# Attention transposes in pairs of 64-row halves, into pairs of PSUM banks, and table clears three stages later

## The chip, the cores and the metric

One core of a Trainium2 chip runs one launch. The metric is device microseconds of that launch; a time is the median of several runs of the same program. The engines are TensorE (PE in the profile; its weight loads are listed apart as PEld), VectorE (DVE), ScalarE (ACT), GpSimd (POOL) and SyncE (SP), which only issues DMAs here.

## The reference

Three layers follow each other. Attention has 2 batches, 8 heads, 576 positions and head size 64, with a relative bias made by a small network; then a mixture of 8 experts of which each token takes one, with a capacity of 288; then a feed-forward layer with a leaky gate.

```python
scores = scale * np.matmul(q, k.transpose(0, 1, 3, 2)) + bias.transpose(2, 0, 1)[None]
attn = np.exp(scores - np.max(scores, axis=-1, keepdims=True))
attn = attn / (np.sum(attn, axis=-1, keepdims=True) + 1e-09)
x = np.matmul(attn, v)                       # -> (1152, 512), all heads side by side
logits = x @ w_gate; expert_idx = np.argmax(logits, axis=1)
h = np.maximum(np.einsum('ecd,edf->ecf', disp, w1), 0.0)
y = np.einsum('ecf,efd->ecd', h, w2)         # rows go back to their tokens, times a gate
h = x @ w_in
out = (np.maximum(h, 0.0) + alpha * np.minimum(h, 0.0)) @ w_out
```

## The kernel before

Everything is float32. Attention is cut into units: a batch, a pair of heads `hp`, and one or two blocks of 128 query rows (`uls`); the last 64 rows of both heads of a pair make a small unit. `SL` lists 24 stages of units: stages 0 to 3 are small units, 4 to 11 single units (one block), 12 to 23 double units (two blocks a and b; at stages 12, 13, 18 and 20 a small unit stands ahead in the list). In the double stages no bias work is left; the single and small ones carry two blocks of it each (`bias_mm`, `bias_out`).

`course` (L886) writes out the order of TensorE, ScalarE and VectorE by hand (`manual_schedule`). In stage s it runs the scores of unit u of this stage and the transposes and values of unit w of the stage before:

- `scores` (L227): matmuls of 64 rows each, the two heads in the two 64-row halves of the array, 288 columns each, into two PSUM tiles of the pool `pq` (two buffers of two banks). A float32 matmul shows as two weight loads and two matmuls.
- `low` (L250, VectorE): adds the bias, writes the exponent's argument to SBUF and its row minimum; it releases the PSUM tile.
- `expo` (L258, ScalarE): the exponential, with the row sum.
- `turn` (L272): TensorE transposes blocks of 128 x 128 (9 blocks of keys for each block of rows: 4 of head 0, one in the middle that holds the end of both heads, 4 of head 1) into a one-bank tile of the pool `pt`, and returns the copy of it to `PT` in SBUF by ScalarE ('A') or VectorE ('D').
- `values` (L292): probabilities times values, 64-column tiles, into the pool `pa`, and VectorE's copy to `xT`.

In a double stage the order is: scores of a, their two `low`; the transposes of w (18 blocks in five tiles, three copied by ScalarE, two by VectorE) and those of a waiting small unit (5 blocks in two tiles); a step of `late`; `expo` of a, scores of b, and their `low`; values; `expo` of b; a step; the scores, `low` and `expo` of a small unit of this stage; a step. `late` is a list of the work that follows attention, by steps: from stage 18 on the first batch's routing (`logits` to `gates`), `row` (L450: four transposes give 128 tokens' rows of x, VectorE scales them), `scatter`, `second` (gathers the first expert's rows and loads its weights), `first_halves` and `rows_in` (L878: transposes the gathered rows).

PSUM has eight banks: `pq` four, `pt` three tiles of one bank, `pa` one. `pt` also takes the tiles of routing and rows. `LD` lists what SP loads at which stage: bias tables, keys/queries/values (`load`, four buffers), and `clear` (L117), which stores zeros to the table of scattered rows (four stores) and to the output (three), one at each of stages 14 to 20. The scatter waits for the first four. SP's, POOL's and the later engines' order outside `course` is made by a scheduler.

Of the kernel before, what the change touches and what calls it, by code (L numbers as in the profile page):

```python
# [10 lines left out]
F32 = mybir.dt.float32  # L11
# [4 lines left out]
ALU = mybir.AluOpType  # L16
AX = mybir.AxisListType
ET = mybir.EngineType
PSUM = bass.MemoryType.PSUM
# [20 lines left out]
def build(tc, nc, a):  # L40
    V, A, G, T, SY = nc.vector, nc.scalar, nc.gpsimd, nc.tensor, nc.sync
    with contextlib.ExitStack() as ctx:
        left, right = contextlib.ExitStack(), contextlib.ExitStack()

        def pool(stack, name, bufs=1, **k):
            return stack.enter_context(tc.tile_pool(name=name, bufs=bufs, **k))
# [9 lines left out]
        pt = pool(banks, "pt", 3, space=PSUM)  # L56
        pa = pool(banks, "pa", 1, space=PSUM)
        ps1 = lambda p, name, *s: p.tile([128, *(s or (512,))], F32, tag="pt" if p is pt else "pa", name=name)
# [151 lines left out]
        def unit(b, hp, *uls):  # L210

            u = Unit()
            u.b, u.hp, u.small, u.uls = b, hp, not uls, uls
            return u
# [51 lines left out]
        def copy(e, o, i):  # L266
            if e == 'A':
                A.copy(o, i)  # L268
            else:
                V.tensor_copy(o, i)  # L270

        def turn(u, *js):  # L272

            if u.small:
                t = ps1(pt, "t1", 4, 128)
                if js[0] == 0:
                    u.PT = ap.tile([128, 5, 128], F32, tag="pt4", name="pt4", bufs=2)
                    for j in range(4):
                        T.transpose(t[:, j], u.P[:, 128 * j:128 * j + 128], ident)
                    return lambda: copy('A', u.PT[:, 0:4], t)  # L280
                T.transpose(t[:, 0], u.dup.rearrange("p a b -> p (a b)"), ident)
                return lambda: [copy('D', u.PT[p, 4, 0:64], t[p, 0, p]) for p in halfs]
            n = 128 * len(u.uls)
            if js[0] == 0:
                u.PT = ap.tile([128, 9, 256], F32, tag="PT", name="PT")
            t = ps1(pt, "t1", 512 // n, n)
            for jl, j in enumerate(js):
                for i, ul in enumerate(u.uls):
                    T.transpose(t[:, jl, 128 * i:128 * i + 128], u.P[ul][:, 128 * j:128 * j + 128], ident)  # L289
            return lambda e: copy(e, u.PT[:, js[0]:js[-1] + 1, :n], t[:, 0:len(js)])  # L290
# [57 lines left out]
        def routing(b):  # L348
# [101 lines left out]
            def row(u):  # L450
                t = ps1(pt, "xp")
                for hp in range(4):
                    T.transpose(t[:, 128 * hp:128 * hp + 128], xT[b][:, hp, 128 * u:128 * u + 128], ident)
                x = r.x[u] = raw.tile([128, RW], F32, tag="xr", name="xr", bufs=5)
                V.tensor_tensor(x[:, 0:DM].rearrange("p (h d) -> p h d", h=8), t.rearrange("p (h d) -> p h d", h=8),
                                r.rinv[:, u].unsqueeze(2).to_broadcast([128, 8, 64]), ALU.mult)
                V.tensor_copy(x[:, DM:RW], r.gt[:, u])

            def scatter():
                for u in range(5):  # L460
# [7 lines left out]
                    + tuple(lambda u=u: row(u) for u in range(5)) + (scatter,))]  # L468
# [417 lines left out]
        def course():  # L886
# [31 lines left out]
            for s in range(14, 21):  # L918
                LD[s].append((clear, 3 * s - 42))
# [18 lines left out]
            for s in range(NU + 1):  # L938
# [11 lines left out]
                if u is None or len(u.uls) == 2:  # L950
# [31 lines left out]
                else:  # L982
# [4 lines left out]
                    if w and w.small:  # L987
                        turn(w, 0)()
                        turn(w, 4)()
# [29 lines left out]
        banks.close()  # L1019
        pt = pool(ctx, "pt", 2, space=PSUM)  # L1020
# [194 lines left out]
```

## Time and profile before

| | us |
|---|---|
| median of 3 runs | 391.95 (390.59 to 392.08) |
| profiled execution | 392.17 |
| its span, first to last instruction | 390.1 |
| TensorE matmul busy | 364.9 |
| VectorE busy | 280.2 |
| ScalarE busy | 233.3 |

The span is what the trace covers; the execution's own time lies a little above it. Busy matmul time counts a matmul from its start to its modelled end, and matmuls overlap, so the pace of a group is read from the distance of starts and not from the length of one.

### The profile page before, as it was taken

The page shows a single profiled execution, that of the slowest core. Times are in us where ns is not written, and L with a number is a line of the kernel's source. Part 1 is how long each engine was busy: PE and PEld are TensorE (multiplying, and loading weights), DVE is VectorE, ACT ScalarE, POOL GpSimd, SP SyncE. Part 2 cuts the span into 40 slices and gives each one's busy share as a digit, 9 for nine tenths or more (in the row PEclk, how much of TensorE's full clock was granted, in tenths as well). Part 3 has the DMA queues.
Part 4 walks back from the last instruction along what each step waited for, and adds up shares of the span by engine and source line. Part 5 has one row for each costly group of instructions (what it writes and reads, how often), then busy time and mean ns, then how long its engine had stood idle before and what let it go on. Part 6 is the DMA issues. An engine that isn't in the chain of part 4 may idle for free. (4 is left out here: it accounts for less than half of the span.)

```text
span 390.1 us, 7650 instructions
## 1 busy us (share of the span) xinstructions
PE 364.9 (94%) x2784; PEld 272.4 (70%) x2785; DVE 280.2 (72%) x680; ACT 233.3 (60%) x525; POOL 29.8 (8%) x48
## 2 busy tenths in 40 slices
PE   4989999999999999899999988999999999999993
PEld 2424566666666657577669877778889898988982
DVE  5988868746566656867759898216999999879430
ACT  4877798886566644555754326334866765755531
POOL 1000000000000000023022340002000000000004
PEclk9999999999999999999999999999999999999997
DMA  7898996789999960520765199483454755550003
GB/s 311 228 282 295 363 294 202 256 274 360 313 357 361 402 228 0 186 102 9 229 170 181 52 279 347 133 276 103 159 172 152 215 163 163 163 164 1 0 2 134
DMA packets 44011, 78.79 MB, mean 202 GB/s; under 512 B 7127, under 2 KB 21591, under 8 KB 43964
## 3 DMA queue, kind: packets, MB, share of 16 engines
q1 hardware_dynamic: 42780, 75.73, 60.3%
q0 software_dynamic: 1184, 2.48, 1.7%
q8 instruction: 24, 0.39, 0.4%
q14 instruction: 23, 0.19, 0.2%
HBM read 59.50 MB, written 20.09 MB: 204 GB/s over the span
## 5 line engine op out<-in xcount | busy, mean ns | idle before, releaser
L254 DVE CUSTOM_DVE_ANT_0 p<-sps,bias 128x576 f32<-128x576 f32 x72 | 52.0, 755 | 26.5 <-PE sps L247 12.7
L261 ACT ACTIVATE p<-p,mn 128x576 f32<-128x576 f32 x72 | 56.0, 781 | 23.3 <-DVE mn L254 23.3
L247 PE MATMUL sps<-kqv 64*128 64x288 f32 x256 | 47.9, 432 | 2.5 <-DVE mn L254 1.9
L171 DVE TENSOR_SCALAR h<-c 128x528 f32<-128x528 f32 (+17 forms) x126 | 46.4, 443 | 0.2
L179 PE MATMUL bps<-h,c 128*32 128x512 f32 (+17 forms) x352 | 36.1, 498 | 7.7 <-DVE h L171 5.5
L289 PE MATMUL t<-ident,p 128*128 128x128 f32 x288 | 39.1, 281 | 1.2 <-ACT PT L268 0.9
L289 PEld LDWEIGHTS t<-ident,p 128*128 128x128 f32 x288 | 30.7, 141 | 12.5 <-issue 5.8
L268 ACT COPY PT<-t 128x512 f32<-128x512 f32 (+2 forms) x59 | 25.6, 506 | 21.1 <-PE t L289 21.1
L247 PEld LDWEIGHTS sps<-kqv 64*128 64x128 f32 x256 | 26.0, 185 | 16.2 <-issue 4.2
L819 PE MATMUL fg<-yh,w1l 128*128 128x304 f32 x120 | 36.3, 302 | 0.0
L819 PE MATMUL fg<-yh,w1h 128*128 128x304 f32 x120 | 36.3, 302 | 0.0
L819 PE MATMUL fg<-yl,w1h 128*128 128x304 f32 x120 | 36.2, 302 | 0.0
L187 ACT ACTIVATE st<-bps,c 128x527 f32<-128x527 f32 (+35 forms) x72 | 31.2, 515 | 4.4 <-PE bps L179 4.4
L310 PE MATMUL av<-PT,kqv 128*64 128x256 f32 (+1 forms) x320 | 32.8, 343 | 0.0
L744 ACT ACTIVATE cv<-d 128x512 f32<-128x512 f32 x32 | 21.6, 674 | 16.0 <-DMA d<-in_wout 5.4
L310 PEld LDWEIGHTS av<-PT,kqv 128*64 128x64 f32 x320 | 19.7, 136 | 14.9 <-issue 5.2
L831 PE MATMUL facc<-w2h,hl 128*128 128x512 f32 (+1 forms) x75 | 29.7, 396 | 0.0
L831 PE MATMUL facc<-w2l,hh 128*128 128x512 f32 (+1 forms) x75 | 29.6, 394 | 0.0
L831 PE MATMUL facc<-w2h,hh 128*128 128x512 f32 (+1 forms) x75 | 29.5, 394 | 0.0
L179 PEld LDWEIGHTS bps<-h,c 128*32 128x32 f32 x352 | 12.6, 114 | 23.8 <-DVE h L171 7.8
L514 ACT CAST hh<-g 128x304 fp32r<-128x304 f32 x32 | 14.3, 446 | 15.8 <-DVE g L823 15.8
L819 PEld LDWEIGHTS fg<-yh,w1h 128*128 128x128 f32 x120 | 22.6, 188 | 1.0
(200 smaller groups left out, 743.4 us busy)
## 6 DMA issues: line engine op xcount, KB each, us to landing
bias<-bd SPq DMA_DIRECT2D x24, 576.0 KB, 6.3
kqv<-in_kqv SPq DMA_DIRECT2D x14, 864.0 KB, 7.0
bd<-st SPq DMA_DIRECT2D x36, 295.5 KB, 5.7
raw<-in_ew SPq DMA_DIRECT2D x16, 512.0 KB, 6.9
d<-in_win SPq DMA_DIRECT2D x16, 512.0 KB, 3.8
d<-in_wout SPq DMA_DIRECT2D x16, 512.0 KB, 3.4
w<-in_ew SPq DMA_DIRECT2D x6, 512.0 KB, 8.8
xd<-zr SPq DMA_DIRECT2D x4, 722.8 KB, 10.2
```

What stands on the lines that cost most here:

```text
L171: V.tensor_scalar(h, tab[:, :n], psi[:, i:i + 1], 0.0, ALU.add, ALU.max)
L179: T.matmul(ps[32 * c:32 * c + 32, n0:n1], w2n, hs[c][:, n0:n1], start=True, stop=True)
L187: A.activation(st[:, o:o + src.shape[1]], src, AF.Copy, scale=rr[:, t:t + 1])
L247: T.matmul(u.sc[ul, h][0][:, nh, :288], q[p, 128 * ul:128 * ul + 128], k[p, 288 * nh:288 * nh + 288], start=True, stop=True)
L254: V.tensor_tensor_reduce(out.rearrange("p (a b) -> p a b", a=2), ps[:, :, :288], bias.rearrange("p (a b) -> p a b", a=2), -0.125, 3.0e38, ...
L261: A.activation(out, out, AF.Exp, bias=mn, scale=-1.0, accum_out=acc)
L268: A.copy(o, i)
L289: T.transpose(t[:, jl, 128 * i:128 * i + 128], u.P[ul][:, 128 * j:128 * j + 128], ident)
L310: T.matmul(o[p, c], v[:, j, p], rhs(h, j), start=j == 0, stop=False, skip_group_check=True)
L744: A.mul(v, r[:, :, 1].bitcast(F32), 2.0 ** -112)
L819: T.matmul(ps, w[:, 128 * k:128 * k + 128], x[:, k, s], start=k + i == 0, stop=k + i == 5)
L831: T.matmul(acc[i][:m], h[:, r:r + m], w, start=f == 0 and j == 0, stop=f == NF - 1 and j == 2)
```

## The change

`turn` transposes each 128 x 128 block as two halves of 64 rows, with a 64 x 64 identity; half h goes to bank h of a tile of two banks. So the array is tiled as for the scores. The tiles are one pool now, `pt` and `pa` being the same ring of two buffers of two banks. In a double stage the middle keys come first (ScalarE copies them), then keys 0 to 3 and keys 5 to 8, of which ScalarE copies half 0 and VectorE half 1. ScalarE's first exponential of a stands between these copies. The small unit's transposes, in one tile of five blocks, and the first step of `late` come after the scores of b. `row` of the first batch uses the same halves, rows 0 and 1 and rows 3 and 4 in one tile each, and moves by a step or two in `late`. The seven clears go to stages 17 to 23.

```diff
-        pt = pool(banks, "pt", 3, space=PSUM)
-        pa = pool(banks, "pa", 1, space=PSUM)
+        pt = pa = pool(banks, "pt", 2, space=PSUM)
+        packed = True
+        ps2 = lambda name: pt.tile([128, 2, 512], F32, tag="pt", name=name)
+
+        def ps1(p, name):
+            if packed:
+                return ps2(name)[:, 0]
+            return p.tile([128, 512], F32, tag="pt" if p is pt else "pa", name=name)
...
+            t = ps2("t1")
...
+                rows = [u.P[ul][:, 128 * j:128 * j + 128] for j in js for ul in u.uls]
+            for i, x in enumerate(rows):
+                for h, p in enumerate(halfs):
+                    T.transpose(t[:, h, 64 * i:64 * i + 64], x[p], ident[p, p])
+            src = t[:, :, 0:64 * len(rows)].rearrange("p h (m c) -> p h m c", c=64)
...
+            def out(*es):
+                if len(es) == 1:
+                    copy(es[0], dst, src)
+                else:
+                    for h, e in enumerate(es):
+                        copy(e, dst[:, h], src[:, h])
+            return out
...
-            for s in range(14, 21):
-                LD[s].append((clear, 3 * s - 42))
+            for s in range(17, 24):
+                LD[s].append((clear, 3 * s - 51))
...
                     if len(w.uls) == 2:
-                        for js, e in (((0, 1), 'A'), ((2, 3), 'A'), ((4,), 'A'), ((5, 6), 'D'), ((7, 8), 'D')):
-                            turn(w, *js)(e)
+                        turn(w, 4)('A')
+                        if u:
+                            expo(u, u.uls[0], 0)
+                        turn(w, 0, 1, 2, 3)('A', 'D')
+                        turn(w, 5, 6, 7, 8)('A', 'D')
                     else:
-                        for js, e in (((0, 1, 2, 3), 'A'), ((4,), 'A'), ((5, 6, 7, 8), 'D')):
-                            turn(w, *js)(e)
-                    if wsmall:
-                        turn(wsmall, 0)()
-                        turn(wsmall, 4)()
-                    step()
+                        turn(w, 0, 1, 2, 3, 4)('A')
+                        expo(u, u.uls[0], 0)
+                        turn(w, 5, 6, 7, 8)('A')
                     if u:
-                        expo(u, u.uls[0], 0)
                         scores(u, u.uls[1])
                         expo(u, u.uls[0], 1)
                         low(u, u.uls[1], 0)
                         low(u, u.uls[1], 1)
+                    if wsmall:
+                        turn(wsmall)()
+                    step()
                     c = values(*[z for z in (w, wsmall) if z])
...
-                        turn(w, 0, 1, 2, 3)('A')
-                        turn(w, 4)('A')
+                        turn(w, 0, 1, 2, 3, 4)('A')
                         turn(w, 5, 6, 7, 8)('A')
...
-                    late.extend([[], st[:1], [], st[1:3], st[3:5], [], st[5:7], st[7:8], st[8:9], st[9:11], [], [],
-                                 st[11:13], [], [st[13], st[14], second], [], [first_halves], [], [rows_in]])
+                    late.extend([[], st[:1], [], st[1:3], st[3:5], [], st[5:7], st[7:8], st[8:9], [], st[9:10], [],
+                                 st[10:11], st[11:12], [st[12], second], [], [first_halves], [], [rows_in]])
```

## Rows read from the trace of the kernel before

**Rows 1.** The page: busy us, share of span and instructions of each engine.

```profile
PE 364.9 (94%) x2784; PEld 272.4 (70%) x2785; DVE 280.2 (72%) x680; ACT 233.3 (60%) x525; POOL 29.8 (8%) x48
```

**Rows 2.** Windows: stretch, length, busy PE/PEld/DVE/ACT/POOL (x), clock, DMA share, GB/s.

```profile
79.83:85.51 5.68, 5.68 (x56) 3.48 (x54) 1.74 (x5) 5.06 (x15) 0.00 (x0) 1.00 0.86 260
...
118.83:125.90 7.07, 7.05 (x57) 4.65 (x55) 4.60 (x11) 4.50 (x12) 0.00 (x0) 1.00 1.03 344
...
174.32:182.91 8.59, 8.57 (x70) 5.91 (x66) 6.40 (x17) 4.50 (x11) 1.96 (x2) 1.00 0.08 27
...
199.93:385.50 185.57, 178.10 (x1147) 157.99 (x1144) 140.53 (x290) 99.75 (x211) 17.43 (x18) 1.00 0.50 154
```

**Rows 3.** Single lines' instructions, durations in ns: min/median/max, first to last start.

```profile
L289 PEld LDWEIGHTS t<-ident,p x288: 137/141/146, 48.0 to 192.5; 128*128 128x128 f32 x144
L289 PE MATMUL t<-ident,p x288: 272/273/332, 48.0 to 192.6; 128*128 128x128 f32 x144
...
L247 PE MATMUL sps<-kqv x256: 402/403/507, 41.1 to 187.3; 64*128 64x288 f32 x128
...
L310 PE MATMUL av<-pt,kqv x128: 219/222/270, 32.2 to 174.0; 128*64 128x64 f32 x128
```

**Rows 4.** Timeline, stage 16: start, length, engine, line, tiles, count, [idle before].

```profile
118.83 1.24 PE L247 MATMUL sps<-kqv 64*128 64x288 f32 x8
...
120.00 2.48 PE L289 MATMUL t<-ident,p 128*128 128x128 f32 x18
...
120.20 0.76 DVE L254 CUSTOM_DVE_ANT_0 p<-sps,bias 128x576 f32<-128x576 f32 x1 [0.82 <-PE sps L247]
...
120.88 0.75 DVE L254 CUSTOM_DVE_ANT_0 p<-sps,bias 128x576 f32<-128x576 f32 x1
121.34 0.91 PEld L289 LDWEIGHTS t<-ident,p 128*128 128x128 f32 x8 [0.26 <-ACT PT L268]
...
122.03 1.29 DVE L270 COPY PT<-t 128x512 f32<-128x512 f32 x2 [0.39 <-PE t L289]
...
122.42 1.24 PE L247 MATMUL sps<-kqv 64*128 64x288 f32 x8
...
123.59 1.95 PE L310 MATMUL av<-PT,kqv 128*64 128x256 f32 x16
```

**Rows 5.** Timeline, stage 13 and the start of stage 14.

```profile
92.88 1.24 PE L247 MATMUL sps<-kqv 64*128 64x288 f32 x6 [0.33 <-DVE mn L254]
...
94.47 0.75 DVE L254 CUSTOM_DVE_ANT_0 p<-sps,bias 128x576 f32<-128x576 f32 x1
...
97.19 1.24 PE L247 MATMUL sps<-kqv 64*128 64x288 f32 x8
...
100.57 0.64 PE L310 MATMUL av<-pt,kqv 128*64 128x64 f32 x16
...
101.25 1.19 PE L237 MATMUL sps<-kqv 64*64 64x288 f32 x8
...
103.45 1.23 PE L247 MATMUL sps<-kqv 64*128 64x288 f32 x6 [0.33 <-DVE mn L254]
```

**Rows 6.** Timeline, stage 11, a single stage.

```profile
79.83 1.54 PE L247 MATMUL sps<-kqv 64*128 64x288 f32 x8
...
82.05 1.24 ACT L268 COPY PT<-t 128x512 f32<-128x512 f32 x3 [0.62 <-PE t L289]
```

**Rows 7.** Timeline, stage 24, the end of attention.

```profile
189.98 1.31 PE L289 MATMUL t<-ident,p 128*128 128x128 f32 x10
...
193.20 0.37 PEld L567 LDWEIGHTS xjT<-ident,xj 96*128 96x128 f32 x4 [0.15 <-DVE PT L270]
...
194.28 1.51 PE L310 MATMUL av<-PT,kqv 128*64 128x256 f32 x10
```

**Rows 8.** DMA issues, 111.7 to 126: count, KB each, median us to landing.

```profile
kqv<-in_kqv SPq DMA_DIRECT2D x3, 864.0 KB, 8.7
out<-zr SPq DMA_DIRECT2D x3, 768.0 KB, 10.3
```

More of the change, by code (lines that the diff above doesn't have):

```diff
@@ L55, in build @@
         banks = contextlib.ExitStack()
-        pt = pool(banks, "pt", 3, space=PSUM)
-        pa = pool(banks, "pa", 1, space=PSUM)
-        ps1 = lambda p, name, *s: p.tile([128, *(s or (512,))], F32, tag="pt" if p is pt else "pa", name=name)
+        pt = pa = pool(banks, "pt", 2, space=PSUM)
[5 more added lines that the diff above has]
+            return p.tile([128, 512], F32, tag="pt" if p is pt else "pa", name=name)
         class Table:
@@ L213, in unit @@
             u.b, u.hp, u.small, u.uls = b, hp, not uls, uls
+            u.first = 4 if len(uls) == 2 else 0
             return u
@@ L272, in turn @@
         def turn(u, *js):
+            t = ps2("t1")
             if u.small:
[L275 to L290, printed above, removed]
+                u.PT = ap.tile([128, 5, 128], F32, tag="pt4", name="pt4", bufs=2)
@@ new lines, in turn @@
+                rows = [u.P[:, 128 * j:128 * j + 128] for j in range(4)] + [u.dup.rearrange("p a b -> p (a b)")]
+            else:
+                if js[0] == u.first:
+                    u.PT = ap.tile([128, 9, 256], F32, tag="PT", name="PT")
+                rows = [u.P[ul][:, 128 * j:128 * j + 128] for j in js for ul in u.uls]
+            for i, x in enumerate(rows):
+                for h, p in enumerate(halfs):
+                    T.transpose(t[:, h, 64 * i:64 * i + 64], x[p], ident[p, p])
@@ new lines, in turn, with out @@
+            src = t[:, :, 0:64 * len(rows)].rearrange("p h (m c) -> p h m c", c=64)
+            if u.small:
+                def out():
+                    copy('A', u.PT[:, 0:4].rearrange("p m (h c) -> p h m c", h=2), src[:, :, 0:4])
+                    for h, p in enumerate(halfs):
+                        copy('D', u.PT[p, 4, 0:64], src[p, h, 4])
+                return out
+            dst = u.PT[:, js[0]:js[-1] + 1, :128 * len(u.uls)]
+            if len(u.uls) == 2:
+                dst = dst.rearrange("p j (i h c) -> p h (j i) c", h=2, c=64)
+            else:
+                dst = dst.rearrange("p j (h c) -> p h j c", h=2)
@@ L292, in values @@
+            def out(*es):
+                if len(es) == 1:
+                    copy(es[0], dst, src)
+                else:
+                    for h, e in enumerate(es):
+                        copy(e, dst[:, h], src[:, h])
+            return out
         def values(*us):
@@ L448, in routing, with row @@
             r.x = {}
[L450 to L457, printed above, removed]
+            def row(*us):
+                t = ps2("xp") if packed else ps1(pt, "xp")
+                for i, u in enumerate(us):
+                    x = r.x[u] = raw.tile([128, RW], F32, tag="xr", name="xr", bufs=5)
+                    if packed:
+                        c = 256 * i
+                        for hp in range(4):
+                            for h, p in enumerate(halfs):
+                                T.transpose(t[:, h, c + 64 * hp:c + 64 * hp + 64], xT[b][p, hp, 128 * u:128 * u + 128],
+                                            ident[p, p])
+                        z = x[:, 0:DM].rearrange("p (g h d) -> p h g d", h=2, d=64)
+                        y = t[:, :, c:c + 256].rearrange("p h (g d) -> p h g d", d=64)
+                        w = r.rinv[:, u].rearrange("p (g h) -> p h g", h=2).unsqueeze(3).to_broadcast([128, 2, 4, 64])
+                    else:
+                        for hp in range(4):
+                            T.transpose(t[:, 128 * hp:128 * hp + 128], xT[b][:, hp, 128 * u:128 * u + 128], ident)
+                        z, y = [z.rearrange("p (h d) -> p h d", h=8) for z in (x[:, 0:DM], t)]
+                        w = r.rinv[:, u].unsqueeze(2).to_broadcast([128, 8, 64])
+                    V.tensor_tensor(z, y, w, ALU.mult)
+                    V.tensor_copy(x[:, DM:RW], r.gt[:, u])
             def scatter():
@@ L467, in routing @@
                     (logits, logits_rows, choose, highest, hot, ranks, slots, places, gates)
-                    + tuple(lambda u=u: row(u) for u in range(5)) + (scatter,))]
+                    + tuple(lambda u=u: row(*u) for u in (((0, 1), (2,), (3, 4)) if b == 0 else ((0,), (1,), (2,), (3,), (4,)))) + (scatter,))]
         jl = gp.tile([128, 52], I32, name="jl")
@@ L1019, in build @@
         banks.close()
+        packed = False
         pt = pool(ctx, "pt", 2, space=PSUM)
```

3 lines of the change are left out of this document (1 added, 2 removed).

## The prediction

> **What bounds the kernel now.** I read the page first: TensorE is recorded busy for 94% of the span [rows 1]. Such a number is an average, so next I cut the trace into stages. In the windows view the attention's plain double stage (one unit of two 128-row blocks, no routing) takes 7.07 us with TensorE busy 7.05, VectorE 4.60, ScalarE 4.50, at a granted clock of 1.00 (2.4 GHz) [rows 2]. So these stages are bound by the order of TensorE's own work, and a shorter TensorE step can shorten them until something else is late. The single stages (5.68 us, TensorE 5.68 [rows 2]) look alike, but there the timeline shows ScalarE idle 0.62 us until the transposes arrive [rows 6], and little else of its time free: a loop of ScalarE through TensorE. From 199.93 on, 185.57 us [rows 2] belong to experts and feed-forward, whose code is not touched. I leave them as they are.
>
> Within a double stage the timeline [rows 4] gives, from the scores of block a at 118.83 (call it 0): transposes 1.17 to 3.6, scores of block b from 3.59, values from 4.76, next stage at 7.07.
>
> **What a transpose costs, before and after.** 18 transposes took 2.48 us [rows 4]. The last lasts 0.273, and the first 0.332, some 0.06 over the median, which is its exposed weight load [rows 3]. The reader should separate duration from pace: ten weight loads and eight in two runs, with a wait of 0.2 between them; (0.91 - 0.141)/7 = 0.110 us per transpose [rows 3, 4]. The scores' pairs, already in 64-row halves, stream 288 columns in (1.24 - 0.403 - 0.104)/3 = 0.244 us for two matmuls at once [rows 3, 4]. That is 0.85 ns a column, and 128 columns at 0.85 are 0.109: the transpose is paid by its 128 streamed identity columns, not by its load of about 0.06.
>
> After the change a block is two transposes of 64 rows with 64 streamed columns each. No row shows a transpose in halves. Upper bound: the halves don't overlap and loads aren't hidden, 2 x (0.06 + 0.054) = 0.23 us a block. Middle: they don't overlap but loads hide, 0.11. Lower bound: they overlap as the scores' halves do. The nearest row for that is the small unit's values, pairs of 64-column matmuls with two loads each: 16 in 0.64, so (0.64 - 0.222)/7 = 0.060 a pair [rows 3, 5]. I take 0.060, because the row tiling is that of the scores, whose halves do run together, and because load (0.06) and stream (0.054) both fit.
>
> The tiling stays that of the scores, so the change of tiling disappears on both sides. From the end of the scores' stream (118.83 + 0.104 + 4 x 0.244 = 119.91) to the first transpose's effective start (120.00 + 0.06) there are 0.15 us, and on the other side about 0.2 [rows 4].
>
> **A plain double stage.** TensorE's work alone would shrink by 18 x 0.050 + 0.35 + the 0.2 wait = 1.45 us. It can't all be had. Scores of b need the two PSUM buffers that VectorE's reductions read. Those start at 120.20 and the second ends at 120.88 + 0.75 = 121.63, 2.80 after the stage's start [rows 4]. New sequence: scores of a to 1.08; middle keys (2 blocks) to 1.20; keys 0 to 3 to 1.68; keys 5 to 8 reuse the middle keys' buffer, whose copy ScalarE ends at about 1.9, so they run 1.95 to 2.45 (a new wait of 0.25; behind it on TensorE stand scores of b, which wait longer for VectorE anyway); scores of b not before 2.87 (VectorE); stream end 3.94; values need VectorE's two copies (1.29 together [rows 4]) from 2.81 to 4.10, so they start about 4.16. Before, the values' first effective start was 4.81 (4.76 and a 0.05 load) and the stage ended 2.25 later; 4.16 + 2.25 = 6.41, **0.65 less**. ScalarE's order (middle copy, exponential, two half copies, exponential; a copy of 512 takes it about 0.5, by three in 1.24 [rows 6]) ends its copies at 4.02, just in time. Four such stages (15 to 18): 2.6.
>
> A rule of the Trainium skill, TensorEngine Tiling (Array Packing), PSUM Bottleneck, speaks against taking the whole 1.45: tiling speeds the matmuls and not the evacuation of PSUM, which may become the bottleneck. By the rule the stage gains 0.65, by TensorE's own time 1.45; the VectorE rows agree with the rule.
>
> **Stages with a small unit's transposes.** In stage 13 scores of a really start at 92.88 (0), VectorE ends its second reduction at 94.47 + 0.75 = 95.22 (2.35), but scores of b start at 97.19 (4.31), because 18 + 5 transposes stand before them [rows 5]. Now they start at 2.48 (transposes, with the buffer wait) and the small unit's five blocks follow (0.3); values at 3.9 run 2.16, small values 0.58 (100.57 + 0.58), the small scores at 6.73, and the next stage's scores 2.20 after these as now (101.25 to 103.45 [rows 5]): 8.93 against 10.57, **1.65 less**. Stage 14, the same without the last part: 1.6. Stage 19: the logits' tile is put between, so values share the buffer of the small transposes, whose VectorE copies now stand behind the reductions of b (to about 5.65): 1.2. Stage 21: as 14, plus rows 0 and 1 in halves behind the values, 8 x 0.05 and a tiling change: 2.2. Sum 6.65.
>
> **The rest of attention.** Stage 12: scores of b already start when VectorE is done; 0. Stage 20: VectorE's routing arithmetic stands ahead of the reductions; 0.2. Stage 22 (8.59 [rows 2]): reductions 0.35 later because of rows 0 and 1, scores of b 3.25, values 4.7 to 6.86, rows 3 and 4 to 7.5: 1.1. Stage 23: VectorE's rows 3 and 4 delay its reductions and, through the exponentials, the last transposes: 0. Single stages 5 to 11: ScalarE's copy now starts 0.55 after the scores' stream instead of 0.84 (82.05 against 79.83 + 1.54 - 0.403 + 0.244 = 81.21 [rows 3, 6]), and two copies replace three (0.05): 0.33 x 7 = 2.3, well inside the 0.62 idle. Small stages 1 to 4: 0.4 in all.
>
> **What it costs.** One ring of two buffer pairs replaces three banks and one. After the last scores, the row transposes for the first expert already wait for VectorE's copies [rows 7]. With two buffers they and the values wait for each other: the first can start when the copies of keys 0 to 3 are done (3.2 after the last transposes of attention began at 189.98), the third after the first one's split, the values behind the second's split, 5.6 against 4.3 (194.28 - 189.98 [rows 7]). I charge 1.3. If the scheduler hides it behind logits: 0.
>
> **Moved clears.** Seven stores (the last three of 768 KB [rows 8]), each one instruction on SP's queue, leave stages 14 to 20 for 17 to 23; POOL's clearing of their source tile moves with the first, and nothing stands behind it there. The key and value loads take 8.7 us to land [rows 8] and are issued two stages ahead (14.1 us); after two shortened stages there are 12.8. So the clears weren't holding anything, and nothing is gained. Behind them on SP stand the loads of stages 17 to 23, then the gathered rows and expert weights. The scatter waits for the first four, issued some 20 us ahead. Price nothing; if the last three collide with the first expert's weights, 768 KB at the 344 GB/s of a busy stage [rows 2] is 2.2 us each, of which one may count.
>
> **Sum.** 6.65 + 2.6 + 1.3 + 2.3 + 0.4 - 1.3 = 11.95. The profiled execution took 392.17 (span 390.1 and 2.1 around it), 0.2 over the median of 391.95. 392.17 - 11.95 = **380.2 us**.
>
> **Rivals.**
> - *Halves don't overlap* (0.11 a block). For it: no row shows them. Against: the scores' halves do. Plain stages lose only 0.17 each, stages with small units 0.8, singles 0.2, the rest 1.5: 6.8 less gain, **387**.
> - *Slower: halves neither overlap nor hide their loads* (0.23). Eighteen blocks then take 4.1, scores of b start at 5.2 instead of 3.59, and each plain stage is 1.6 longer, small-unit stages 1.8, singles 0.35, rows and small stages 4: **about 413**. It turns slower at about 0.13 us a block. Against it: loads run ahead of matmuls in every row of these groups.
> - *VectorE isn't late*: the whole 1.45 in double stages, **373**. Against: its reductions' rows can't shorten.
> - *Ring of two decides*: the second transposes wait for a copy that ScalarE reaches only after an exponential; scores of b at about 3.9, and then plain stages gain nothing and the others half: **387 to 391**. For it: before, the transposes already wait 0.2 for a copy [rows 4]. Against: the middle copy stands first on ScalarE, idle by then.
>
> **How the numbers follow.** Forecast 0.60 (own range 377 to 384); no overlap 0.13; ring 0.12; all gained 0.05; slower 0.07; the rest, clears or a queue, 0.03. The range 375.5 to 388.5 leaves out the slower case, half of the ring's, and the fastest. A measurement of this kernel can tell about 0.5% (2 us) from no change: faster 0.84, within 0.08, slower 0.08.
>
> **What would show it.** Transposes as 64 x 128 pairs, 36 in about 1.1 us of work; no gap after the scores; scores of b waiting for VectorE and not for TensorE; plain stages of 6.4; stage 13's distance 8.9; single stages of 5.35; from the last transposes to the first expert 1.3 longer; 185.6 us unchanged. It is wrong if the pace of a block is 0.11 or more, or if TensorE waits for ScalarE's or VectorE's copies ahead of the values by over 0.5.

## The result, and the profile after

The changed kernel takes 386.55 us (median), the kernel before, on the same chip, 392.01: a ratio of 0.986, with a 95% interval of 0.983 to 0.990. The gain is 5.5 us where 12 were forecast. One of the four executions took 392.88 us at a mean granted clock of 0.974, where the others had 0.993 to 0.995, and is left out of the ratio. The profiled execution took 386.03, with a span of 384.1 (390.1 before), so the trace shows 6.0 us to be explained.

I cut both traces at the first scores of each stage, as for the prediction. A stage's length is the distance from there to the next stage's scores.

| stretch | before | forecast | after | e1_whole | e10_banks | e16_banks_late |
|---|---|---|---|---|---|---|
| start to stage 5 (prelude, small units, stage 4) | 46.05 | 45.65 | 44.83 | 44.41 | 44.77 | 44.73 |
| stages 5 to 11, together | 39.44 | 37.1 | 37.12 | 36.78 | 37.15 | 37.15 |
| 12 | 6.30 | 6.30 | 6.69 | 6.68 | 6.48 | 6.30 |
| 13 (units of 5 + 18 blocks) | 10.57 | 8.92 | 9.52 | 9.09 | 8.96 | 8.97 |
| 14 | 9.40 | 7.80 | 8.31 | 7.82 | 7.75 | 7.75 |
| 15, plain | 7.06 | 6.41 | 7.15 | 6.25 | 6.34 | 6.34 |
| 16, plain | 7.06 | 6.41 | 7.15 | 6.34 | 6.43 | 6.43 |
| 17, plain | 7.06 | 6.41 | 7.15 | 6.52 | 7.38 | 6.43 |
| 18, plain and a small unit's scores | 9.97 | 9.32 | 10.05 | 9.22 | 9.30 | 9.33 |
| 19 | 10.91 | 9.71 | 10.13 | 9.59 | 9.21 | 9.21 |
| 20 | 9.15 | 8.95 | 9.18 | 8.87 | 8.87 | 8.88 |
| 21, with rows 0 and 1 | 11.34 | 9.14 | 10.62 | 10.12 | 10.06 | 10.05 |
| 22 | 8.60 | 7.50 | 8.66 | 8.46 | 8.19 | 7.99 |
| 23 and 24, to the first expert | 17.01 | 18.31 | 16.77 | 17.93 | 15.46 | 15.10 |
| first expert to the end | 190.21 | 190.2 | 190.77 | 190.93 | 193.56 | 190.77 |
| span | 390.1 | 378.2 | 384.1 | 379.0 | 379.9 | 375.4 |

(The last three columns are experiments, told below.) The singles came out as forecast. The plain double stages, which were to lose 0.65 each, became 0.09 longer, and stages 12 to 22 together gave 2.8 instead of 10.55. So these stages miss 7.8 us of the forecast and the stretch behind the first expert 0.6, while the start and stages 23 and 24 are 0.8 and 1.5 shorter than forecast.

The page of the changed kernel (busy us, share of the span, instructions) and the windows of two plain stages and of what follows the attention (length, then busy time and count of each engine, granted clock, DMA share, GB/s):

```profile
span 384.1 us, 8342 instructions
## 1 busy us (share of the span) xinstructions
PE 351.6 (92%) x3132; PEld 264.0 (69%) x3133; DVE 279.3 (73%) x679; ACT 233.6 (61%) x518; POOL 29.2 (8%) x48
...
113.61:120.77 7.16, 6.91 (x74) 4.51 (x73) 4.51 (x11) 4.60 (x12) 0.00 (x0) 1.00 1.04 382
120.77:127.92 7.15, 6.90 (x74) 4.50 (x73) 4.51 (x11) 4.59 (x12) 0.00 (x0) 1.00 1.02 405
193.33:384.10 190.77, 178.74 (x1148) 157.39 (x1144) 140.90 (x290) 99.26 (x211) 17.27 (x18) 0.99 0.50 151
```

TensorE's busy time fell by 13.3 us against [rows 1], though the span fell by only 6. So TensorE's work did shrink as meant, and more than half of it turned into waiting. In a plain stage it is now busy 6.91 of 7.16 (7.05 of 7.07 in [rows 2]). The timeline of stage 16 shows where it waits (start, us, engine, line, operation, in brackets the idle time before it and who ended it):

```profile
113.61 1.24 PE L253 MATMUL sps<-kqv 64*128 64x288 f32 x8
...
114.69 1.47 PE L290 MATMUL t<-ident,p 64*128 64x64 f32 x36
114.89 0.76 DVE L260 CUSTOM_DVE_ANT_0 p<-sps,bias 128x576 f32<-128x576 f32 x1 [0.74 <-PE sps L253]
115.01 0.37 ACT L274 COPY PT<-t 128x256 f32<-128x256 f32 x1 [1.36 <-PE t L290]
...
115.57 0.75 DVE L260 CUSTOM_DVE_ANT_0 p<-sps,bias 128x576 f32<-128x576 f32 x1
115.75 0.78 ACT L267 ACTIVATE p<-p,mn 128x576 f32<-128x576 f32 x1 [0.36 <-DVE mn L260]
...
116.39 0.78 PEld L253 LDWEIGHTS sps<-kqv 64*128 64x128 f32 x6 [0.15 <-DVE mn L260]
...
116.52 1.05 ACT L274 COPY PT<-t 128x512 f32<-128x512 f32 x2
117.12 1.29 DVE L276 COPY PT<-t 128x512 f32<-128x512 f32 x2 [0.79 <-ACT PT L274]
...
117.87 2.32 PE L330 MATMUL av<-PT,kqv 128*64 128x256 f32 x15 [0.25 <-DVE PT L276]
...
118.46 1.27 PEld L330 LDWEIGHTS av<-PT,kqv 128*64 128x64 f32 x13 [0.41 <-DVE PT L276]
```

Read it from the top. The 36 halves follow the scores without a gap, and scores of b wait for VectorE's reduction until 116.39, 2.78 into the stage (forecast 2.87). Up to here it is the forecast. Then VectorE, which has been free since 116.3, waits until 117.12 for *ScalarE*, and starts when the first of ScalarE's two half copies is over. Its copies begin 3.51 into the stage instead of 2.81, and TensorE's values wait for them. The same wait, of 0.79, stands in every double stage from 14 to 23, and of 0.73 in 13; in stage 21 the small unit's transposes wait behind it as well (0.69). In the kernel before, VectorE's copies waited for TensorE's transposes and not for ScalarE (0.39 [rows 4]). This is the line on which the result turns. It has two possible causes, since both engines read one pair of PSUM banks and both write one SBUF tile in interleaved pieces of 64 columns.

Three smaller waits are new. In the order of the timeline's rows: in stage 8 VectorE waits for a load of constants; in stage 12 the values wait for a copy of ScalarE that stands behind an exponential; and in stage 21 two rows share a pair of banks, so that the second row's transposes wait until VectorE has read the first.

```profile
61.41 0.17 DVE L466 COPY gt<-c 128x5 f32<-128x5 f32 x1 [2.19 <-DMA c<-in_c]
...
86.29 0.74 PEld L330 LDWEIGHTS av<-PT,kqv 128*64 128x64 f32 x13 [0.22 <-ACT PT L274]
...
166.86 0.68 DVE L488 TENSOR_TENSOR xr<-xp,rinv 128x512 f32<-128x512 f32 x1
...
167.60 0.47 PE L478 MATMUL xp<-ident,xT 64*128 64x64 f32 x8 [0.86 <-DVE xr L488]
```

### The profile page after: what moved, and what is told of

Same layout as the page of the kernel before. It is cut to its first block, busy times and chain, and to the rows that moved or that the text cites. A ratio compares the mean times of both kernels' runs of the same rounds, so it can differ in the third digit from the quotient of the medians.

```text
span 384.1 us, 8342 instructions
## 1 busy us (share of the span) xinstructions
PE 351.6 (92%) x3132; PEld 264.0 (69%) x3133; DVE 279.3 (73%) x679; ACT 233.6 (61%) x518; POOL 29.2 (8%) x48
## 5 line engine op out<-in xcount | busy, mean ns | idle before, releaser
L253 PE MATMUL sps<-kqv 64*128 64x288 f32 x256 | 50.7, 429 | 2.5 <-DVE mn L260 1.9
L253 PEld LDWEIGHTS sps<-kqv 64*128 64x128 f32 x256 | 28.3, 186 | 15.8 <-DVE mn L260 5.0
L274 ACT COPY PT<-t 128x512 f32<-128x512 f32 (+2 forms) x52 | 26.8, 549 | 19.4 <-PE t L290 19.4
L330 PE MATMUL av<-PT,kqv 128*64 128x256 f32 (+1 forms) x320 | 35.5, 344 | 2.1 <-DVE PT L276 1.2
L290 PEld LDWEIGHTS t<-ident,p 64*128 64x128 f32 x640 | 28.9, 139 | 10.5 <-DVE PT L276 2.7
L290 PE MATMUL t<-ident,p 64*128 64x64 f32 x640 | 32.9, 227 | 2.9 <-DVE xT L334 1.2
L330 PEld LDWEIGHTS av<-PT,kqv 128*64 128x64 f32 x320 | 20.8, 136 | 17.7 <-DVE PT L276 6.4
L184 PEld LDWEIGHTS bps<-h,c 128*32 128x32 f32 x352 | 12.2, 115 | 23.6 <-DVE mn L260 8.9
```

The source lines that it names most:

```text
L184: T.matmul(ps[32 * c:32 * c + 32, n0:n1], w2n, hs[c][:, n0:n1], start=True, stop=True)
L253: T.matmul(u.sc[ul, h][0][:, nh, :288], q[p, 128 * ul:128 * ul + 128], k[p, 288 * nh:288 * nh + 288], start=True, stop=True)
L290: T.transpose(t[:, h, 64 * i:64 * i + 64], x[p], ident[p, p])
L330: T.matmul(o[p, c], v[:, j, p], rhs(h, j), start=j == 0, stop=False, skip_group_check=True)
```

## The experiments

Each starts from the changed kernel unless said otherwise. The time before on the same chip was 392.02 for the first four (e1, e2, e3, e6), 392.17 for e7, e10, e13 and e14, and 391.37 for the others.

### What VectorE's copy waits for: e1_whole, e2_apart, e10_banks

**e1_whole** takes the question away: each pair of banks is copied whole by one engine, so nothing is shared.

```diff
-                        turn(w, 0, 1, 2, 3)('A', 'D')
-                        turn(w, 5, 6, 7, 8)('A', 'D')
+                        turn(w, 0, 1, 2, 3)('D')
+                        turn(w, 5, 6, 7, 8)('A')
```

> The changed kernel, but in the double stages each pair of banks is copied whole by one engine: keys 0 to 3 by VectorE, keys 5 to 8 by ScalarE. Theory (VectorE's half copy waits until ScalarE's half copy of the same keys has ended, because both write interleaved columns of one SBUF region): without that, VectorE copies right after its second reduction, 2.8 us into a plain stage and not at 3.5, values start at about 4.15 instead of 4.85, the plain stage falls from 7.15 to 6.4 us, stages with a small unit's transposes by 0.5 each: 380 to 381 us in all. Rival (the copies simply need that time, or ScalarE is the limit): plain stage 7.1, 386.5 us.

Measured: 380.88 us, ratio 0.974 (0.970 to 0.978); plain stages 6.25, 6.34 and 6.52. So the two half copies cost what the forecast missed. Why one waits for the other is still open.

**e2_apart** keeps the half copies and lays the destination out by half, so that the two engines write separate regions; the values read it strided.

```diff
+                    u.PH = u.PT.rearrange("p a b -> p (a b)").rearrange("p (h j n) -> p h j n", h=2, j=9)
...
-                dst = dst.rearrange("p j (i h c) -> p h (j i) c", h=2, c=64)
+                dst = u.PH[:, :, js[0]:js[-1] + 1].rearrange("p h j (i c) -> p h (j i) c", c=64)
```

> The changed kernel with its half copies kept (half 0 by ScalarE, half 1 by VectorE), but PT of a double unit laid out as half, key, row, so that the two halves land in separate stretches of SBUF; values read it through a stride. Theory (the wait comes from the interleaved destination): VectorE's first half copy starts at 2.8 us and not behind ScalarE's at 3.5, plain stage 6.4, stages with a small unit 0.6 shorter each, 380 us. Rival (the wait comes from the shared PSUM pair, whichever its banks): VectorE still starts behind ScalarE, plain stage 7.15, 386.5 us. If values pay for the strided read, the plain stage grows by what the ten pairs lose.

Measured: 388.51 us, ratio 0.992 (0.990 to 0.995), ten executions of 385.18 to 390.72; in the profiled one, the 385.18, the plain stage is still 7.15. In its timeline the wait is unchanged to the hundredth:

```profile
116.10 1.05 ACT L274 COPY PT<-t 128x512 f32<-128x512 f32 x2
116.70 1.29 DVE L276 COPY PT<-t 128x512 f32<-128x512 f32 x2 [0.79 <-ACT PT L274]
```

My first theory, the interleaved destination, falls.

**e10_banks** leaves the destination interleaved and gives each half a one-bank PSUM tile of its own (two rings of two instead of one ring of two pairs). Where one engine copies both halves it now needs two instructions.

```diff
-        ps2 = lambda name: pt.tile([128, 2, 512], F32, tag="pt", name=name)
+        ps2 = lambda name: [pt.tile([128, 512], F32, tag=n, name=name) for n in ("pt", "pu")]
...
-                    T.transpose(t[:, h, 64 * i:64 * i + 64], x[p], ident[p, p])
+                    T.transpose(t[h][:, 64 * i:64 * i + 64], x[p], ident[p, p])
```

> The two halves of a block go to two one-bank PSUM tiles instead of one two-bank tile; ScalarE and VectorE still copy one half each into the same interleaved destination. Theory (the pair tile orders the two engines' copies): VectorE's half copy of keys 0 to 3 starts about 2.9 us into a plain double stage instead of 3.51, the values follow about 0.6 us earlier, a plain stage takes 6.4 to 6.6 instead of 7.15, stages 13, 14, 19 and 21 lose about 0.6 each too, and the whole kernel takes 380 to 382.5. Rival (the destination's interleaving, or the two engines getting in each other's way in PSUM itself): VectorE's copy still starts at 3.5 or lasts longer by as much, the plain stage stays 7.15, the kernel 386 to 388.

Measured: 382.31 us, ratio 0.975 (0.969 to 0.980); stages 15 and 16 take 6.34 and 6.43, where 6.41 was forecast. In the timeline of its stage 16 (scores of a at 111.45) VectorE's copies start 2.73 in, with no wait, beside ScalarE's:

```profile
114.18 1.28 DVE L276 COPY PT<-t 128x512 f32<-128x512 f32 x2
...
114.39 1.05 ACT L274 COPY PT<-t 128x512 f32<-128x512 f32 x2
...
115.48 1.82 PE L328 MATMUL av<-PT,kqv 128*64 128x256 f32 x14
```

Both pairs of copies last as long as in the changed kernel (1.28 and 1.05 against 1.29 and 1.05), so no disturbance of one engine by the other shows. The cause is the shared pair tile: VectorE's copy waited for ScalarE's because both read one PSUM tile, and not because of the interleaved data or because both engines read PSUM at once. That is shown. That a semaphore of ScalarE's copy is what held it is the profile's inference.

### What the halves themselves are worth: e6_full

e1_whole again with whole 128x128 transposes: order of keys, ring, row pairs and everything else stay those of the changed kernel.

```diff
-            for i, x in enumerate(rows):
-                for h, p in enumerate(halfs):
-                    T.transpose(t[:, h, 64 * i:64 * i + 64], x[p], ident[p, p])
+            t = t.rearrange("p b c -> p (b c)").rearrange("p (m c) -> p m c", c=128)
+            for i, x in enumerate(rows):
+                T.transpose(t[:, i], x, ident)
```

> The halves alone undone: attention's transposes are 128 x 128 again, four to a bank, in the changed kernel's order and ring of buffer pairs, copied whole as in e1_whole (keys 0 to 3 by VectorE, 5 to 8 by ScalarE). Theory (order and ring alone bring little, halves bring TensorE 0.05 us a block and the change of tiling): scores of b start at 3.4 us in a plain stage, values at 4.7, stage 6.95; stages with a small unit about 1 us longer than in e1_whole, single stages 0.2; 388 to 390 us. Rival (the new order and not the halves shortens the kernel): as e1_whole within 1 us.

Measured: 390.65 us, ratio 0.996 (0.992 to 1.000). Its plain stage takes 6.77 and its stages 5 to 11 together 39.48. So the halves are worth 9.8 us between this kernel and e1_whole (390.65 - 380.88). By the traces 9.0 of it lies in stages 5 to 22 (134.77 against 125.74). The new order and ring alone, with whole copies, shorten a plain stage by 0.29 (7.06 to 6.77) and the singles not at all.

### The second row behind the first: e3_rows and e13_fill

**e3_rows** puts both rows' transposes ahead of both of VectorE's scalings.

```diff
-                    V.tensor_tensor(z, y, w, ALU.mult)
-                    V.tensor_copy(x[:, DM:RW], r.gt[:, u])
+                    todo.append((x, z, y, w, u))
+                for x, z, y, w, u in todo:
+                    V.tensor_tensor(z, y, w, ALU.mult)
+                    V.tensor_copy(x[:, DM:RW], r.gt[:, u])
```

> The changed kernel, but where two rows share a pair of banks, the transposes of both stand ahead of VectorE's two scalings. Theory (the second row's transposes wait 0.9 us for VectorE to read the first row out of the same banks, and TensorE with them): the row steps at the ends of stages 21 and 22 fall from 1.6 us to 0.8 each, 385.0 us. Rival (VectorE's scalings set the end of those stages anyway, because its reductions come later): the wait moves into the next stage, 386.5 us.

Measured: 387.53 us, ratio 0.990 (0.986 to 0.993): no gain. Stages 21 and 22 do shrink, by 1.09 and 0.24, so the wait was there. But stages 23 and 24 take 20.51 instead of 16.77. About 0.9 of that is VectorE: both scalings now stand in front of stage 23's reductions, which start 2.09 after the scores (173.69, 175.78) instead of 1.22 (176.56, 177.78). The rest, 2.8, stands in the windows of e3_rows before the first expert (columns as above):

```profile
182.00:185.20 3.20, 1.66 (x37) 1.31 (x36) 2.81 (x6) 2.41 (x6) 0.00 (x0) 1.00 0.86 240
185.20:187.80 2.60, 2.26 (x12) 1.53 (x12) 1.69 (x3) 0.96 (x2) 0.00 (x0) 0.64 1.05 358
187.80:192.50 4.70, 4.57 (x21) 2.19 (x20) 0.64 (x2) 1.37 (x2) 0.00 (x1) 0.50 0.34 123
```

The last column but two is the granted clock. It fell from 1.00 (2.4 GHz) to 0.50 (1.2 GHz) and the last 16 values took 3.68 us; in the changed kernel's trace the same 16 took 1.95 at 1.00. Just before it fell, at 186, TensorE had twice stood idle between runs of transposes, as its timeline shows:

```profile
183.11 1.22 PE L290 MATMUL t<-ident,p 64*128 64x64 f32 x32 [0.66 <-DVE xT L334]
185.23 1.45 PE L602 MATMUL xjT<-ident,xj 96*128 96x96 f32 x8 [0.91 <-DVE PT L276]
186.94 0.90 PE L602 MATMUL xjT<-ident,xj 96*128 96x96 f32 x4 [0.26 <-DVE xl L550]
187.84 3.68 PE L330 MATMUL av<-PT,kqv 128*64 128x256 f32 x16
```

**e13_fill** fills these places with transposes that nobody reads (they add work and leave nothing out).

```diff
+                for _ in range(fill[r]):
+                    T.transpose(warm[:, 0, 0:128], ident, ident)
...
-            job_transpose(J.xj, J.x)
+            job_transpose(J.xj, J.x, fill=(10, 0, 6))
```

> As e3_rows, with ten 128x128 transposes of the identity, whose result nobody reads, ahead of the first expert's row transposes and six ahead of the last of them, where TensorE waits anyway. Theory (e3_rows lost its gain because the granted clock fell to 0.50 at 186 us, and it fell after those waits): the clock stays at 1.00 up to the first expert, stages 23 and 24 take 17.0 to 17.6 together instead of 20.5, and the kernel 384.5 to 385.7. Rival (the order of the rows itself costs the end, whatever the clock): stages 23 and 24 stay above 19, the kernel 387 to 388.

Measured: 385.15 us, ratio 0.982 (0.976 to 0.987). The clock stayed at 1.00 there and the values took 1.95, but stages 23 and 24 took 18.03, above my 17.0 to 17.6, as VectorE's 0.9 was not in the expectation. Between the rows' order and the changed kernel little is left: 1.3 gained in stages 21 and 22, 1.3 given back behind them.

Is the clock a property of the program or of the execution? The changed kernel and e5_clear14 (below) issue the same instructions in the same order on every engine (six of TensorE's 3132, which overlap their neighbours, start up to three places apart). In the trace of the first, with the waits of 0.66, 0.91 and 0.56 us, the clock stayed at 1.00; in the second, with 0.66, 0.90 and 0.52, it fell. First the changed kernel's windows, then e5_clear14's:

```profile
187.00:189.00 2.00, 1.39 (x12) 0.90 (x11) 1.40 (x3) 0.96 (x2) 0.00 (x0) 1.00 1.02 360
189.00:191.00 2.00, 1.95 (x19) 1.31 (x20) 0.62 (x2) 0.48 (x1) 0.00 (x0) 1.00 0.97 341
```

```profile
188.00:190.00 2.00, 1.48 (x9) 1.19 (x9) 1.01 (x3) 0.96 (x2) 0.00 (x0) 0.50 1.00 345
190.00:192.00 2.00, 2.00 (x10) 1.34 (x12) 1.11 (x2) 0.48 (x1) 0.00 (x0) 0.50 0.81 300
```

Stages 23 and 24 took 16.77 in the one and 19.25 in the other: 2.5 us from the clock alone. So the row before the expert is a place where it may fall, not one where it must. In the traces without added transposes it fell in this stretch in e1_whole, e3_rows, e5_clear14, e7_c1 and e15_late, and not in the changed kernel, e2_apart, e6_full, e10_banks and e16_banks_late; in the three with them it didn't. That is consistent with the filling, but three traces where half fall anyway are no proof.

### Stage 8's load: e7_c1

The token constants are loaded in the prelude instead of in the turn of stage 12.

```diff
-            LD[12] += [(lambda: SY.dma_start(c1, a["c1"]),), (rest_sums, 0)]
+            LD[12] += [(rest_sums, 0)]
...
                     load_vd(0)
+                    SY.dma_start(c1, a["c1"])
```

> The load of the token constants is issued in the prelude instead of in stage 12's turn. Theory (stage 8's 6.26 us comes from VectorE waiting 2.19 us for that load): stage 8 takes 5.3, stages 9 and 10 go from 4.95 and 5.06 to 5.3, the net gain is 0.3 to 0.5 us: 386.0 to 386.3. Rival (the load only stands for something else that is late there): stage 8 stays 6.2 and the time 386.5; and if the singles' whole gain had been held up by it, 385.5.

Measured: 386.30 us, ratio 0.986 (0.980 to 0.992). Stage 8 takes 5.27, and 9 and 10 take 5.33 each. That fits, but it does not show that the edit did it: in most traces with the load in its old place (e1, e2, e3, e5 and e15 among them) stage 8 is 5.26 or 5.27 too. The wait stands in the changed kernel's trace and in e13_fill's (6.10) and in no other, and the stages after it give most of it back (4.95 and 5.06 in both).

### The clears: e5_clear14, e15_late, e16_banks_late

**e5_clear14** undoes that part of the change alone.

```diff
-            for s in range(17, 24):
-                LD[s].append((clear, 3 * s - 51))
+            for s in range(14, 21):
+                LD[s].append((clear, 3 * s - 42))
```

> Only the part with the clears is undone: they stand at stages 14 to 20 of the loop again instead of 17 to 23. If the scheduler places them anyway, SyncE issues the clears at the same places as in the changed kernel (first at 92.5, last at 120.8 us) and one look gives 386 to 388. If the move did hold them back, they are issued some 20 us earlier or the input loads of stages 14 to 18 land later, and stages 14 to 18 lengthen.

One execution: 389.56 us. Stages 9 to 22 differ from the changed kernel's by 0.4 at most (0.37 and 0.27 in 9 and 10, behind stage 8's load), 12 to 22 by 0.01. SyncE issues the clears in the same order and at the same places: the first 3.87 us into stage 13 here (93.63 - 89.76), 3.86 in the changed kernel (92.50 - 88.64), and 3.87 in the kernel before too (95.67 - 91.80). The rows of the first clear, in the kernel before, the changed kernel and e5_clear14:

```profile
95.67 0.52 SPq L127 DMA_DIRECT2D xd<-zr  x1
```

```profile
92.50 0.54 SPq L132 DMA_DIRECT2D xd<-zr  x1
```

```profile
93.63 0.53 SPq L132 DMA_DIRECT2D xd<-zr  x1
```

The scheduler, which orders SyncE's queue itself, undoes the three stages, so this part of the diff does nothing. The 3.5 us between the two profiled executions (389.56 and 386.03) are in the main the clock, which fell here from 31 to 34 us and from 188 to 195.

**e15_late** holds the clears back in fact, by making the zeros that they send depend on a late value.

```diff
                 zr = raw.tile([128, RW], F32, name="zr")
+                u = SL[17][-1]
+                G.tensor_copy(zr[:, 0:1], xT[u.b][:, u.hp, 128 * u.uls[0]:128 * u.uls[0] + 1])
...
+            for r in range(7):
+                LD[max(20, 16 + r)].append((clear, 3 * r))
```

> The changed kernel with the clears really held back: the zeros that they send are written only after a value of stage 18's output, so that they are issued after the last key loads, from about 132 us. If clears cost nothing in the changed kernel, as the prediction had it: the loads land up to 6 us earlier, no stage moves by more than 0.1, 386 to 387. If TensorE does wait behind them somewhere: 385 to 386. If the late clears hold up the row scatter (168 us) or the first expert's loads: over 387.5.

Measured: 386.50 us, ratio 0.989 (0.983 to 0.996): nothing, as forecast for the clears; stages 12 to 22 agree to 0.01. But the loads do move. The DMA view from 103 to 135 us (KB each, median us from issue to landing), first the changed kernel, then e15_late:

```profile
kqv<-in_kqv SPq DMA_DIRECT2D x5, 864.0 KB, 10.8
bias<-bd SPq DMA_DIRECT2D x5, 576.0 KB, 10.4
```

```profile
kqv<-in_kqv SPq DMA_DIRECT2D x5, 864.0 KB, 5.6
bias<-bd SPq DMA_DIRECT2D x5, 576.0 KB, 3.9
```

A key load lands in half the time when no clear stands before it. In the changed kernel TensorE is too slow to notice. In e10_banks it is not: there the median load takes 12.2, the first scores of stage 18 wait for one, and stage 17 takes 7.38. The same DMA view of e10_banks, and the row of its timeline:

```profile
kqv<-in_kqv SPq DMA_DIRECT2D x5, 864.0 KB, 12.2
```

```profile
125.26 0.51 PE L253 MATMUL sps<-kqv 64*128 64x288 f32 x2 [0.87 <-DMA kqv<-in_kqv]
```

**e16_banks_late** is e10_banks with e15_late's edit, and with stage 12's exponential behind both of ScalarE's copies:

```diff
-                        expo(u, u.uls[0], 0)
                         turn(w, 5, 6, 7, 8)('A')
+                        expo(u, u.uls[0], 0)
```

> e10_banks with the clears held back as in e15_late and stage 12's exponential behind both of ScalarE's copies. Theory (in e10_banks stage 18's scores wait 0.87 us for a key load that queues behind the clears): that wait goes, stage 17 takes 6.4 instead of 7.38, stage 12 6.3 instead of 6.48: 380.9 to 381.5 against 382.3. Rival (the load waits for its own buffer, not for the queue): stage 17 stays 7.3, the kernel 382.

Measured: 377.23 us, ratio 0.963 (0.957 to 0.968). Stage 17 takes 6.43 and stage 12 6.30, as expected; the windows show the two plain stages with the DMA no longer full:

```profile
111.23:117.67 6.44, 6.44 (x74) 5.03 (x73) 4.42 (x11) 4.61 (x12) 0.00 (x0) 1.00 0.67 236
117.67:124.10 6.43, 6.43 (x73) 5.03 (x73) 4.42 (x11) 4.61 (x12) 0.00 (x0) 1.00 0.41 138
```

The time is 4 us better than I expected. By the traces 2.8 of the difference to e10_banks lies behind the first expert (193.56 against 190.77), where e10_banks ran at 0.50 from 221 to 228 us and this one at 1.00. Why the clock held is not settled.

### The parts together: e14_best and e17_banks_late_fill

**e14_best** joins the edits of e1_whole, e3_rows, e7_c1 and e13_fill with stage 12's.

> Whole copies by one engine (e1_whole), both rows' transposes ahead of both scalings (e3_rows), the token constants loaded in the prelude (e7_c1), stage 12's exponential behind both of ScalarE's copies, and the added transposes of e13_fill. If the gains add: 380.9 - 1.3 (stages 21 and 22) - 0.4 (constants) - 0.4 (stage 12) - 1.5 (values ahead of the first expert at the full clock) = 377.3, so 376.5 to 378.5. If what comes after is given (the first expert's rows or weights arrive when they arrive): 379 to 381.

Measured: 379.94 us, ratio 0.968 (0.963 to 0.973). Stage 21 takes 9.05, stage 12 6.30 and the first expert starts at 187.22, 6.1 earlier than in the changed kernel; but stage 17 takes 7.99, with 1.61 us of waiting for stage 18's key load, and from the first expert on it takes 194.16, with the clock at 0.50 from 220 to 230 us. The gains don't add. This trace is of an execution of 383.13 us, 3.2 over the median, so the clock's fall in it does not explain the median. The wait for the load may: it would be 1.6 of the 2.6 us by which the median exceeds the 377.3 of added gains, if it is as long in the other executions, which no trace shows.

**e17_banks_late_fill** is e16_banks_late with added transposes in front of all of the experts' row transposes, in a part of their own PSUM tile that they don't use:

```diff
                 t = ps1(pt, "xjT")
+                for _ in range(fill[r]):
+                    T.transpose(t[:, 384:512], ident, ident)
```

> e16_banks_late with transposes of the identity, whose result nobody reads, in front of the experts' row transposes (five in the first expert's, eight and three in those of the later ones), where TensorE waits for rows. Theory (the clock falls to 0.50 behind these waits and costs e10_banks 2.8 us in the second expert): the clock stays at 1.00 there, first expert to end 190.8 instead of 193.6, the kernel 378 to 379.5. Rival (the clock falls for another reason, or the added work costs as much): 380.5 to 382.5.

Measured: 376.27 us, ratio 0.961 (0.956 to 0.966), the fastest of all, and 1.0 below e16_banks_late, with intervals that overlap. The clock stayed at 1.00, but it did in e16_banks_late's trace without the filling too, so this run decides nothing about it. e16_banks_late and e17_banks_late_fill beat both given kernels by 9 us and more.

## Why the prediction was right and wrong

**The pace of a half: right.** 16 pairs of halves in a row took 1.21 us in the changed kernel, the last half lasting 0.223 by its median: (1.21 - 0.223)/15 = 0.066 us a block, forecast 0.060, and 0.110 before [rows 3, 4]. They run together, no change of tiling is left behind the scores, and e6_full gives their worth directly. The rivals without overlap (387, 413) are out, although one of them has the measured time.

```profile
184.69 1.21 PE L290 MATMUL t<-ident,p 64*128 64x64 f32 x32 [0.66 <-DVE xT L334]
```

**Scores of b bound by VectorE: right**, 2.78 against 2.87. TensorE's own 1.45 could not all be had. The Trainium skill's rule from TensorEngine Tiling (Array Packing), PSUM Bottleneck, by which the stage was to gain 0.65, is borne out by e10_banks: 6.34 to 6.43, where TensorE's own saving would have made it 5.6.

**A plain double stage: wrong, and this is the step that failed.** "Values need VectorE's two copies (1.29 together) from 2.81 to 4.10": the length was right (1.29), the start was not. I had listed VectorE's order and ScalarE's order, each alone, and had ScalarE's copies beginning at the right time; I had not asked whether one engine's copy of the tile waits for the other's. The diff shows both copies out of one `t`, and this was to be asked there. In the trace of before each PSUM tile of the attention (`sps`, `t`, `av`) is read by one engine alone, so no row of these could answer; the bounds for it should have been 0 and the length of ScalarE's copy behind its exponential, some 0.7, for every double stage. With separate tiles, forecast and measurement of stages 12 to 18 agree within 0.07 in e16_banks_late. The same wait is in every double stage from 13 on. Stages 12 to 22 are 6.9 us longer in the changed kernel than in e16_banks_late, 0.4 of it stage 12's: this is most of the 7.8 us missing there.

The prediction had named the sign by which it would be wrong ("if TensorE waits for ScalarE's or VectorE's copies ahead of the values by over 0.5") and had a rival of the same time, the ring of two at 387 to 391. But that rival put scores of b at 3.9, and they came at 2.78; and e10_banks has the gain with two buffers in each ring. The ring isn't the cause.

**Rows 0 and 1: wrong.** I costed the second row's transposes by their own time ("8 x 0.05"). Both rows share a pair of banks, so its first transpose waits for VectorE's reading of the first row: 0.86 of idle TensorE in stage 21, and 0.79 for rows 3 and 4. Stage 21 became 0.72 shorter instead of 2.2 (with the half copies' 0.6 in it), and stage 22 nothing instead of 1.1. Even without that wait VectorE gives 0.9 of the 1.3 us back one stage later (e3_rows).

**Stage 12: missed**, +0.39: the exponential between ScalarE's copies. Put behind them it is 0, as forecast.

**Singles: right.** 2.32 against 2.3 for stages 5 to 11, and ScalarE's idle time is still there (0.34 in stage 11 instead of the 0.62 of [rows 6]), so nothing else had become late. The 0.4 of the small stages can't be read: the stretch up to stage 5 is 1.2 shorter, but it takes from 43.65 to 46.30 in runs that don't edit it (e3_rows, e5_clear14).

**The end: the mechanism right, its price zero.** From the last transposes of attention to the values 5.46 us pass (183.66 to 189.12), forecast 5.6, before 4.30 [rows 7]. But the first expert starts 9.67 after those transposes (193.33), before 9.95 (199.93 - 189.98 [rows 2, 7]): now the values run through in 1.95 and the logits come behind them, and what the ring costs is not added to the end. This was the "if the scheduler hides it: 0" of the text.

**The clears: zero, for another reason than mine.** They weren't moved at all. And the 8.7 us for a key load was a row of the slower kernel [rows 8], where the same clears stand further apart in time. In the changed kernel the median in this stretch is 10.8, which leaves room. In e10_banks it is 12.2, and the load that stage 18 waits for took 14.0 (issued at 111.12, landed at 125.12), more than the 12.8 that the prediction allowed.

**The last 190 us: 0.6 longer** without any edit there. A matmul of the feed-forward that starts 138.9 us behind the first expert in the kernel before starts at 137.0 in the changed one, and a later one at 160.4 instead of 160.5. So a lead of 1.9 us is lost between them; why is not known.

## What to carry over

When two engines are to empty one PSUM tile together, look first whether the second one's instruction waits on the first one's semaphore; one tile for each engine costs nothing in banks and made 0.7 to 0.8 us a stage here. Cost an edit by everything that must be over before the next engine can start, the other engine's half included, and not by the instructions' own lengths. And once a bound gives way, look again at loads that had landed just in time: what cost nothing in the slower kernel (a clear ahead of a key load) was 0.9 and 1.6 us in the faster ones.

## What the runs showed of the hardware that I had not expected

Transposes in 64-row halves run two at a time at 0.066 us for a 128x128 float32 block, where a whole one takes 0.110.

TensorE's granted clock can fall to 0.50 for 3 to 10 us in the middle of the kernel. It did so in nine of the thirteen kernels profiled with the new order, and not in the one trace of the kernel before (mean clock 0.994; other executions of it had means from 0.981 to 0.999). Before each fall TensorE had waited, for 0.4 to 2.1 us at a time, either around 28 to 34 us, or between attention and the first expert, or around the row transposes of the first experts (from 207 us). Waits of that length also stand in traces in which the clock held. The same instructions in the same order fell in one execution and not in another, and the fall cost 2.5 us. A gain of a microsecond upstream can vanish in it, so two single traces that differ by 2 us should be compared by their clock before anything else.
